# Weight conversion by way of a PSUM bank, in a kernel of decay attention and a softplus layer

## The chip, the cores and the metric

The kernel runs on one core of a Trainium2 chip. The metric is the device time of one execution in microseconds (us), lower being better. A core has five engines that work side by side, each through its own queue in order: TensorE (PE in the profile; its weight loads are listed apart as PEld), VectorE (DVE), ScalarE (ACT), GpSimd (POOL) and SyncE (SP), which here issues all DMAs. There are two memories on the core: SBUF, and PSUM with eight banks of 2 KB in each of its 128 partitions, into which TensorE writes its products.

## What is computed

The input is q, k and v (4 batches, 8 heads, 768 positions, 64 elements) in float32, and two weight matrices in float64, w_in (512 x 2048) and w_out (2048 x 512). First an attention with a state that decays:

```python
for t in range(S):
    state = gamma[None, :, None, None] * state + np.einsum('bhd,bhe->bhde', k[:, :, t], v[:, :, t])
    y[:, :, t] = scale * np.einsum('bhd,bhde->bhe', q[:, :, t], state)
```

Its output is laid out as x (3072 x 512) and goes through two products with a softplus between them:

```python
h = x @ w_in
g = np.maximum(h, 0.0) + np.log1p(np.exp(-np.abs(h)))
return (g @ w_out).astype(np.float32)
```

## The kernel before

**Attention** is worked off in 48 units: 24 chunks of 128 positions, two halves of four heads each. A unit's parts (load, decay, operands, scores, new state, outputs) lie on a grid of ticks, four ticks from one unit to the next, so that several units are in work at once. The first ten units (WHOLE) multiply in plain float32; the later ones split each operand into two parts that TensorE multiplies faster (F32R). A unit ends when L251 (ScalarE) and L253 (VectorE) write its rows of xh and xl, the two parts of x.

**The layer** is worked off in 12 blocks of 256 rows of x, each in 8 steps over pairs of 128 columns of w_in: 96 steps. `hidden(s)` multiplies 24 times into one tile hp of 2 KB, which is one PSUM bank (L282 to L284). `softplus_1` sets the sign bits on VectorE (L289, reads hp) and takes the softplus on ScalarE (L290). `softplus_2` adds max(h, 0) on VectorE (L294, the last reader of hp), splits the result into gh (ScalarE, L296) and gl (GpSimd, L298). `second(s)` multiplies 12 times into two banks of acc (L312 to L314). In the program's order second(s - 2) stands behind hidden(s). The first two blocks are woven together: five steps of block 0, eight of block 1, then the last three of block 0.

**PSUM** is divided into three pools: ps_h with three banks for hp, ps_o with two for acc, ps_a with three for the attention. A tile's bank is free for the next tile when its last reader has finished: with three banks, hidden(s) waits for L294 of step s - 3.

**The weights** come as 64-bit floats and are turned into 32-bit floats on the chip from their bits. There are 16 groups f of 128 columns, each with a tile of w_in and one of w_out: 32 tiles of 128 partitions x 512 values. Every value is two 32-bit words, low and high. `load_weights(f)` issues two DMAs of 512 KB; from the fourth group on each of them waits for the ScalarE copy (L86) of the same tile three groups earlier (FETCH). `convert_weights(f)` does for each of the two tiles:

- L80, ScalarE: the high words, read as a 32-bit float, times 2 to the power of -112, in place. This moves the exponent.
- L82, VectorE: w = low words shifted right by 29.
- L83, VectorE: w = (high AND sign bit) OR w.
- L84, VectorE: w = (high shifted left by 3) OR w.
- L86, ScalarE: the first F32R part of w. L87, GpSimd: w minus that part, the second one.

The low and high words are read with a step of two words. The tile w lies in SBUF in a pool of two buffers. It is held from L82 until L86 and L87 have read it. `convert_to` and the loop before the first step spread the conversions among the ticks and the first steps. The program's order gives the priority; the compiler's scheduler orders the instructions of each engine from it, and on the chip each engine works off its own list.

Of the kernel before, what the change touches and what calls it, by code (L numbers as in the profile page):

```python
# [13 lines left out]
U32 = mybir.dt.uint32  # L14
AF = mybir.ActivationFunctionType
ALU = mybir.AluOpType

P = 128
# [11 lines left out]
def decay_attention_then_softplus_ffn(ctx: ExitStack, tc: tile.TileContext, q, k, v, w_in, w_out, qtab, vtab, gtab, out):  # L30
    nc = tc.nc
# [11 lines left out]
    attn = ctx.enter_context(tc.tile_pool(name="attn", bufs=1))  # L43
    ffn = ctx.enter_context(tc.tile_pool(name="ffn", bufs=2))
    wts = ctx.enter_context(tc.tile_pool(name="wts", bufs=2))
    ps_h = ctx.enter_context(tc.tile_pool(name="ps_h", bufs=3, space=bass.MemoryType.PSUM))
    ps_o = ctx.enter_context(tc.tile_pool(name="ps_o", bufs=1, space=bass.MemoryType.PSUM))
    ps_a = ctx.enter_context(tc.tile_pool(name="ps_a", bufs=3, space=bass.MemoryType.PSUM))

    nc.scalar.preload_act_table_set("softplus")  # L50
# [21 lines left out]
    def convert_weights(f):  # L72

        n = ND * P
        converts[f] = []
        for nm, bits, to in zip(("win", "wout"), raw.pop(f), (win, wout)):
            words = bits.bitcast(U32).rearrange("p (n t) -> p n t", t=2)
            low, high = words[:, :, 0], words[:, :, 1]

            nc.scalar.activation(high.bitcast(F32), high.bitcast(F32), AF.Copy, scale=2.0**-112)  # L80
            w = wts.tile([P, n], U32, name="w")
            nc.vector.tensor_scalar(w, low, 29, None, op0=ALU.logical_shift_right)  # L82
            nc.vector.scalar_tensor_tensor(w, high, 0x80000000, w, op0=ALU.bitwise_and, op1=ALU.bitwise_or)  # L83
            nc.vector.scalar_tensor_tensor(w, high, 3, w, op0=ALU.logical_shift_left, op1=ALU.bitwise_or)  # L84
            to[f] = const.tile([P, 2, n], F32R, name=f"{nm}hl", tag=f"{nm}{f}")
            converts[f].append(nc.scalar.copy(to[f][:, 0], w.bitcast(F32)).ins)  # L86
            nc.gpsimd.tensor_tensor(to[f][:, 1], w.bitcast(F32), to[f][:, 0].bitcast(F32), op=ALU.subtract)  # L87
# [253 lines left out]
    def convert_to(n):  # L341
        nonlocal loaded, converted
        while converted < min(NF, n):
            convert_weights(converted)
            converted += 1
            if loaded < NF:
                load_weights(loaded)
                loaded += 1
# [6 lines left out]
    while done < ticks_for(0):  # L355
        tick(done)
        done += 1
        if done % 4 == 2:
            if loaded >= FETCH:
                convert_weights(converted)  # L360
                converted += 1
            load_weights(loaded)
            loaded += 1
# [66 lines left out]
```

## Time and profile before

| | |
|---|---|
| median of 3 runs | 724.39 us (724.37 to 725.52) |
| the profiled execution | 725.87 us, of which the span from first to last instruction is 723.9 us |
| granted TensorE clock over the span | 0.988 of full speed |
| TensorE busy | 694.0 us |
| VectorE busy | 478.1 us |
| ScalarE busy | 356.1 us |
| GpSimd busy | 347.2 us |
| conversions | 32 tiles, the first L82 at 8.4 us, the last L84 at 137.4 us |

The profile is of one execution. The groups of instructions say how long each kind is busy, what one takes on the mean, and how long its engine sat idle before it. The slices cut the span into 40 equal parts of 18.1 us and give busy shares in tenths. The chain follows the work that ended last back from the end, at each step to what released it. In the timeline the first number of a row is the start, the second the duration, both in us. [...]

### The profile page before, as it was taken

How to read it: one execution, taken by the hardware profiler on the slowest of the kernel's cores; microseconds unless marked ns; L12 is line 12 of the kernel's file. 1: busy time of each engine (PE TensorE's matmuls, PEld its weight loads, DVE VectorE, ACT ScalarE, POOL GpSimd, SP SyncE). 2: the span in 40 equal slices, each digit the busy share in tenths (PEclk: the TensorE clock that was granted, in tenths of full speed). 3: DMA queues.
4: the chain of work that ended last, by engine and by line, in shares of the span. 5: the costliest groups of instructions: out<-in, count | busy, mean ns of one | idle time of the engine just before them, and what ended most of it. 6: DMA issues, size and time to landing. Idle time of an engine off the chain costs nothing.

```text
span 723.9 us, 13570 instructions
## 1 busy us (share of the span) xinstructions
PE 694.0 (96%) x5056; PEld 629.3 (87%) x5056; DVE 478.1 (66%) x914; ACT 356.1 (49%) x803; POOL 347.2 (48%) x452
## 2 busy tenths in 40 slices
PE   4789798999999999999999999999999999999997
PEld 3577687899999999999999999999999999999996
DVE  4999989866866766655776666655667667544321
ACT  4655545454554645544654654544555554443221
POOL 5778766645435445345345344444434444332221
PEclk9899999999999999999999999999999999999999
DMA  8865543012211211210211211211211111000000
GB/s 243 244 167 158 157 129 106 16 45 59 66 30 24 66 31 24 67 30 23 67 24 29 66 24 30 65 24 30 66 23 30 54 35 24 30 1 1 30 1 29
DMA packets 90674, 42.83 MB, mean 59 GB/s; under 512 B 77297, under 2 KB 85489, under 8 KB 90609
## 3 DMA queue, kind: packets, MB, share of 16 engines
q1 hardware_dynamic: 90608, 41.97, 21.6%
q8 instruction: 40, 0.66, 0.4%
q14 instruction: 26, 0.20, 0.1%
HBM read 35.66 MB, written 6.29 MB: 58 GB/s over the span
## 4 chain that ended last, share of the span: by engine, by line
PE 86%; DVE 7%; POOL 2%; issue 2%; DMA 2%; ACT 1%; SPq 0%; DVEq 0%; ACTq 0%; POOLq 0%
PE hp L282 12%; PE acc L312 12%; PE hp L283 12%; PE hp L284 12%; PE acc L313 12%; PE acc L314 12%; PE sc L165 3%; DVE w L83 2%; DVE w L84 2%; DVE w L82 1%; PE pp L189 1%; PE tp L115 1%; PE tp L117 1%; PE yp L246 1%; PE yp L247 1%
## 5 line engine op out<-in xcount | busy, mean ns | idle before, releaser
L282 PE MATMUL hp<-xh,winhl 128*128 128x256 f32 x768 | 221.7, 290 | 4.3 <-DVE sp L294 3.2
L283 PE MATMUL hp<-xl,winhl 128*128 128x256 f32 x768 | 218.0, 284 | 2.5 <-DVE xl L253 2.5
L284 PE MATMUL hp<-xh,winhl 128*128 128x256 f32 x768 | 218.7, 285 | 0.9 <-POOL winhl L87 0.9
L298 POOL TENSOR_TENSOR gl<-sp,gh 128x512 fp32r<-128x512 f32 x96 | 129.2, 1346 | 116.5 <-ACT gh L296 100.4
L312 PE MATMUL acc<-wouthl,gh 128*128 128x512 f32 x384 | 154.1, 401 | 2.2 <-ACT part L320 2.2
L282 PEld LDWEIGHTS hp<-xh,winhl 128*128 128x128 f32 x768 | 147.1, 192 | 7.5 <-issue 2.0
L313 PE MATMUL acc<-wouthl,gh 128*128 128x512 f32 x384 | 151.1, 393 | 0.0
L283 PEld LDWEIGHTS hp<-xl,winhl 128*128 128x128 f32 x768 | 147.4, 192 | 4.2 <-DVE xl L253 2.8
L314 PE MATMUL acc<-wouthl,gl 128*128 128x512 f32 x384 | 149.9, 392 | 0.0
L284 PEld LDWEIGHTS hp<-xh,winhl 128*128 128x128 f32 x768 | 147.3, 192 | 2.2 <-POOL winhl L87 1.1
L289 DVE TENSOR_SCALAR sp<-hp 128x512 uint32<-128x512 uint32 x96 | 65.6, 684 | 56.7 <-PE hp L284 50.3
L296 ACT CAST gh<-sp 128x512 fp32r<-128x512 f32 x96 | 59.5, 620 | 85.6 <-PE acc L313 43.1
L290 ACT ACTIVATE sp<-sp 128x512 f32<-128x512 f32 x96 | 60.7, 632 | 60.0 <-DVE sp L289 59.3
L107 POOL TENSOR_TENSOR qn<-qn,qtab_sb 128x256 f32<-128x256 f32 x48 | 32.6, 679 | 116.8 <-DMA qn<-in_q_dram 105.2
L314 PEld LDWEIGHTS acc<-wouthl,gl 128*128 128x128 f32 x384 | 72.3, 189 | 15.6
L312 PEld LDWEIGHTS acc<-wouthl,gh 128*128 128x128 f32 x384 | 72.8, 189 | 14.9 <-ACT part L320 2.4
L313 PEld LDWEIGHTS acc<-wouthl,gh 128*128 128x128 f32 x384 | 72.8, 190 | 11.9 <-issue 0.2
L294 DVE SCALAR_TENSOR_TENSOR sp<-hp,sp 128x512 f32<-128x512 f32 x96 | 65.9, 686 | 13.4 <-ACT sp L290 12.3
L137 DVE TENSOR_TENSOR kq<-tp,kq 64x256 fp32r<-64x256 f32 x76 | 32.1, 422 | 58.0 <-ACT kq L135 56.8
L253 DVE TENSOR_TENSOR xl<-yp,xh 64x256 fp32r<-64x256 f32 x96 | 39.9, 416 | 30.7 <-ACT xh L251 29.7
L134 ACT CAST kq<-tp 64x512 fp32r<-64x512 f32 x76 | 44.1, 581 | 21.7 <-PE tp L117 20.5
L251 ACT CAST xh<-yp 64x256 fp32r<-64x256 f32 x96 | 35.0, 365 | 38.4 <-PE yp L247 33.5
(82 smaller groups left out, 1187.2 us busy)
## 6 DMA issues: line engine op xcount, KB each, us to landing
win<-in_moe_w_in_dram SPq DMA_DIRECT2D x16, 512.0 KB, 3.9
wout<-in_moe_w_out_dram SPq DMA_DIRECT2D x16, 512.0 KB, 3.8
kn<-in_k_dram SPq DMA_DIRECT2D x48, 128.0 KB, 2.4
qn<-in_q_dram SPq DMA_DIRECT2D x48, 128.0 KB, 2.8
vn<-in_v_dram SPq DMA_DIRECT2D x48, 128.0 KB, 2.3
out_dram<-o SPq DMA_DIRECT2D x24, 256.0 KB, 2.1
qtab_sb<-in_qtab_dram SPq DMA_DIRECT2D x1, 4.0 KB, 2.3
vtab_sb<-in_vtab_dram SPq DMA_DIRECT2D x1, 4.0 KB, 2.0
```

The source lines that it names most:

```text
L134: nc.scalar.copy(kq[own, :2, par], tp[own])
L282: nc.tensor.matmul(hp[:, k], lhsT=wt[:, 0, d, :], rhs=xh[:, d, :], start=d == 0, stop=False)
L283: nc.tensor.matmul(hp[:, k], lhsT=wt[:, 0, d, :], rhs=xl[:, d, :], start=False, stop=False)
L284: nc.tensor.matmul(hp[:, k], lhsT=wt[:, 1, d, :], rhs=xh[:, d, :], start=False, stop=d == ND - 1)
L289: nc.vector.tensor_scalar(sp.bitcast(U32), hps[s].bitcast(U32), 0x80000000, None, op0=ALU.bitwise_or)
L290: nc.scalar.activation(sp, sp, AF.Softplus)
L294: nc.vector.scalar_tensor_tensor(g, hps.pop(s), 0.0, g, op0=ALU.max, op1=ALU.add)
L296: nc.scalar.copy(gh, g)
L298: nc.gpsimd.tensor_tensor(gl, sps.pop(s), gh.bitcast(F32), op=ALU.subtract)
L312: nc.tensor.matmul(acc[i][t], lhsT=gh[:, k, ts], rhs=wt[:, 0], start=begins and k == 0, stop=False)
L313: nc.tensor.matmul(acc[i][t], lhsT=gh[:, k, ts], rhs=wt[:, 1], start=False, stop=False)
L314: nc.tensor.matmul(acc[i][t], lhsT=gl[:, k, ts], rhs=wt[:, 0], start=False, stop=ends and k == 1)
```

## The change

The three VectorE operations of a conversion no longer all write w. The first two write a new tile wp, of the same size and type, which lies in PSUM in a pool of one bank; the third reads wp and writes w in SBUF. The bank is taken from ps_h, which has two in place of three. The operations themselves, their number, the ScalarE and GpSimd operations after them and the DMAs are the same.

```diff
-    ps_h = ctx.enter_context(tc.tile_pool(name="ps_h", bufs=3, space=bass.MemoryType.PSUM))
+    ps_h = ctx.enter_context(tc.tile_pool(name="ps_h", bufs=2, space=bass.MemoryType.PSUM))
     ps_o = ctx.enter_context(tc.tile_pool(name="ps_o", bufs=1, space=bass.MemoryType.PSUM))
+    ps_w = ctx.enter_context(tc.tile_pool(name="ps_w", bufs=1, space=bass.MemoryType.PSUM))
     ps_a = ctx.enter_context(tc.tile_pool(name="ps_a", bufs=3, space=bass.MemoryType.PSUM))
...
             nc.scalar.activation(high.bitcast(F32), high.bitcast(F32), AF.Copy, scale=2.0**-112)
+
+            wp = ps_w.tile([P, n], U32, name="wp")
             w = wts.tile([P, n], U32, name="w")
-            nc.vector.tensor_scalar(w, low, 29, None, op0=ALU.logical_shift_right)
-            nc.vector.scalar_tensor_tensor(w, high, 0x80000000, w, op0=ALU.bitwise_and, op1=ALU.bitwise_or)
-            nc.vector.scalar_tensor_tensor(w, high, 3, w, op0=ALU.logical_shift_left, op1=ALU.bitwise_or)
+            nc.vector.tensor_scalar(wp, low, 29, None, op0=ALU.logical_shift_right)
+            nc.vector.scalar_tensor_tensor(wp, high, 0x80000000, wp, op0=ALU.bitwise_and, op1=ALU.bitwise_or)
+            nc.vector.scalar_tensor_tensor(w, high, 3, wp, op0=ALU.logical_shift_left, op1=ALU.bitwise_or)
             to[f] = const.tile([P, 2, n], F32R, name=f"{nm}hl", tag=f"{nm}{f}")
```

## The prediction

> **What bounds the kernel now.** I begin with the page: busy time by engine, then the slices.
>
> ```profile
> PE 694.0 (96%) x5056; PEld 629.3 (87%) x5056; DVE 478.1 (66%) x914; ACT 356.1 (49%) x803; POOL 347.2 (48%) x452
> ...
> DVE  4999989866866766655776666655667667544321
> ```
>
> Over the whole span TensorE (PE) is the bound, at 96%. But VectorE's (DVE's) row of slices reads 9 up to slice 6, some 125 us, and 6 or 7 after that: a first stage with another limit. So next I read busy time by stretch (columns: the stretch, its length, each engine's busy time and instruction count, granted TensorE clock, DMA share, GB/s).
>
> ```profile
> 8.00:20.00 12.00, 8.55 (x42) 6.81 (x40) 9.52 (x13) 6.56 (x14) 7.44 (x10) 1.00 1.15 314
> 20.00:140.00 120.00, 104.14 (x669) 89.33 (x667) 115.82 (x142) 64.81 (x135) 88.67 (x89) 0.93 0.50 142
> 140.00:724.00 584.00, 578.96 (x4343) 531.78 (x4341) 352.38 (x758) 282.78 (x653) 248.06 (x343) 1.00 0.14 36
> ```
>
> From 20 to 140 us VectorE is busy 115.8 of 120 us and TensorE is not full: 15.9 us idle, at a clock of 0.93. After 140 us TensorE idles 5.0 of 584 us, tail included. So whatever the change does for conversions it does before 140 us; after that it can only do harm.
>
> What fills VectorE there? The groups by line and shape (busy us, mean ns, idle before):
>
> ```profile
> L83 DVE SCALAR_TENSOR_TENSOR w<-win,w 128x512 uint32<-128x512 uint32 x16 | 21.7, 1356 | 0.8 <-ACT win L80 0.3
> L83 DVE SCALAR_TENSOR_TENSOR w<-wout,w 128x512 uint32<-128x512 uint32 x16 | 20.3, 1267 | 0.5
> L84 DVE SCALAR_TENSOR_TENSOR w<-win,w 128x512 uint32<-128x512 uint32 x16 | 17.6, 1098 | 0.3
> L84 DVE SCALAR_TENSOR_TENSOR w<-wout,w 128x512 uint32<-128x512 uint32 x16 | 17.3, 1080 | 0.3
> L82 DVE TENSOR_SCALAR w<-win 128x512 uint32<-128x512 uint32 x16 | 13.4, 840 | 2.2 <-POOL winhl L87 1.2 <-DMA win<-in_moe_w_in_dram 1.1
> L82 DVE TENSOR_SCALAR w<-wout 128x512 uint32<-128x512 uint32 x16 | 10.5, 654 | 1.3 <-POOL wouthl L87 1.1
> ```
>
> The six groups sum to 100.8 us for 96 passes, 3.15 us for each of 32 tiles. Now the same instructions' own spread (min/median/max ns), from the view of tile w:
>
> ```profile
> L82 DVE TENSOR_SCALAR w<-win x16: 406/480/3925, 8.4 to 133.1; 128x512 uint32<-128x512 uint32 x16
> L83 DVE SCALAR_TENSOR_TENSOR w<-win,w x16: 675/1567/2724, 9.1 to 133.6; 128x512 uint32<-128x512 uint32 x16
> L84 DVE SCALAR_TENSOR_TENSOR w<-win,w x16: 675/983/2211, 9.9 to 136.1; 128x512 uint32<-128x512 uint32 x16
> ```
>
> One shape, a factor of four (L82: nearly ten) between fastest and slowest: these passes wait while they run. For whom, the timeline of both engines shows (start, duration):
>
> ```profile
> 47.44 2.72 DVE L83 SCALAR_TENSOR_TENSOR w<-win,w 128x512 uint32<-128x512 uint32 x1
> ...
> 47.09 0.73 POOL L200 TENSOR_TENSOR td<-td,gtab_sb 64x256 f32<-64x256 f32 x1 [0.96 <-DVE td L197]
> 47.78 1.26 POOL L87 TENSOR_TENSOR wouthl<-w,wouthl 128x512 fp32r<-128x512 f32 x1
> 49.01 0.60 POOL L108 TENSOR_TENSOR vn<-vn,vtab_sb 128x256 f32<-128x256 f32 x1
> ```
>
> L83 sits at 47.44 until GpSimd's (POOL's) three operations are through at 49.61, and ends 0.55 us later. Against it stands the first product's own pass, L294, one operand of which is in PSUM (hp) and one in SBUF (sp):
>
> ```profile
> 52.32 0.69 DVE L294 SCALAR_TENSOR_TENSOR sp<-hp,sp 128x512 f32<-128x512 f32 x1
> ...
> L289 DVE TENSOR_SCALAR sp<-hp x96: 673/681/693, 50.1 to 712.0; 128x512 uint32<-128x512 uint32 x96
> L294 DVE SCALAR_TENSOR_TENSOR sp<-hp,sp x96: 671/691/693, 52.3 to 713.4; 128x512 f32<-128x512 f32 x96
> ...
> 52.15 1.29 POOL L87 TENSOR_TENSOR winhl<-w,winhl 128x512 fp32r<-128x512 f32 x1 [2.54 <-ACT winhl L86]
> ```
>
> It starts inside a GpSimd subtraction and takes its usual 0.69 us; in 96 runs it never exceeds 0.693, though GpSimd is busy half the span. That row carries the forecast.
>
> **The change, part by part.** *L83 and L84.* They come to have one operand in PSUM and one in SBUF, as L294 has. Undisturbed they took 0.675 already; I take 0.69 and no waits. *L82.* Its source stays in SBUF, its target moves to PSUM. No instruction here writes PSUM from VectorE. The near rows are 0.41 (SBUF to SBUF) and 0.68 (L289, the mirror image); I take 0.68, so its best case is lost and so are its waits. Sum: 96 x 0.69 = 66.2 us against 100.8, **34.6 us less VectorE time**, 1.08 per tile.
>
> [...]
>
> *In place in one bank.* L83 reads and writes the same PSUM bank. No row shows that. Below, it is free (0.69, L294); above, reading and writing take turns and the 0.55 us that L83 needed after its wait come twice: 0.69 + 0.55 = 1.24. I take 0.69, the row of the same operation. With the upper end L83 falls only from 42.0 to 39.7, and the sum is 34.6 - 17.6 = 17.0.
>
> *What of it lies on the path.* The chain that ended last, asked up to 112.4 us (from there on it runs on TensorE):
>
> ```profile
> by line: DVE w L83 13.5%; issue 13.2%; DVE w L84 10.3%; DVE w L82 8.7%; DMA win<-in_moe_w_in_dram 3.9%; DMA vn<-in_v_dram 3.4%; POOL wouthl L87 3.3%; DMA wout<-in_moe_w_out_dram 3.0%; DVE xl L253 2.5%; POOL winhl L87 2.5%; DVE sp L294 2.4%;
> ...
> 9.15 0.70 DVE w L83
> ...
> 26.87 1.54 issue
> ...
> 79.24 1.64 issue
> ...
> 87.57 2.37 POOL gl L298
> ...
> 108.95 0.60 DVE sp L294
> 109.55 0.60 DVE w L83
> ```
>
> The three lines hold 32.5% of 112.4 us, 36.5 us, in 43 pieces (the first and the last are shown). Five "issue" pieces (26.87 and 79.24 are the first and last, 6.9 us in all) are the running rest of such a pass: together 43.4. Unhindered passes follow one another every 0.60 us (108.95 to 109.55) and 0.73 where the next needs the last one's result (9.15 to 9.88, L83 to L84); 43 x 0.66 = 28.4. **The path loses 15.0 us.** GpSimd's operations wait for VectorE too (in the chain one of gl takes 2.37 us at 87.57, where the free ones above took 1.26 and 1.29 at the same shape); I add 1.0.
>
> *The ring of the first product.* With two banks, hidden(s) waits for L294 of step s-2, not s-3. First the wait as it is with three banks (us in all, times, longest), then in the traced order the first matmul of a step against the pass that would free its bank with two:
>
> ```profile
> PE hp L282 <- DVE sp L294: 3.2, 2, 1.7
> ...
> 105.01 0.28 PE L282 MATMUL hp<-xh,winhl 128*128 128x256 f32 x1
> ...
> 108.87 0.68 DVE L294 SCALAR_TENSOR_TENSOR sp<-hp,sp 128x512 f32<-128x512 f32 x1
> ...
> 326.54 0.28 PE L282 MATMUL hp<-xh,winhl 128*128 128x256 f32 x1
> ...
> 320.39 0.69 DVE L294 SCALAR_TENSOR_TENSOR sp<-hp,sp 128x512 f32<-128x512 f32 x1
> ```
>
> Step 7 began 4.5 us before L294 of step 5 was done; steps 8, 10, 11, 18 and 19 were early by 5.1, 0.6, 2.6, 0.2 and 0.5 in the same reckoning: 13.6 us that two banks would take at old durations. In the steady part there is room (step 38: 5.5 us; the least after step 19 is 1.8), so nothing is lost there. Queued behind the waiting matmul are all of TensorE's later ones, second(s-2) with them; queued ahead of L294 on VectorE are mostly conversion passes, three or four of them. At 0.36 us less each L294 comes about 1.3 us earlier; what is gained by the same cause shifts both sides. I charge **2 us**, ends 0 and 13.6.
>
> *The rest at nothing.* wp has one bank; its next writer, L82, follows L84 on the same queue, so no other engine waits. L84, not L82, now waits for a free w (bufs=2, freed by L87): 2.3 us of idle before L82 today; w is held two passes less, and what is queued behind L84 is the same as behind L82. Cover for this is GpSimd's slack; it is busy 88.7 of 120 us, so it is what is late next. The weight loads wait for L86 of three groups earlier and will be asked for sooner; DMA moved 314 GB/s from 8 to 20 us and 142 from 20 to 140, so it can follow. No instruction or DMA is added.
>
> Sum against the profiled execution (725.87 us, span 723.9): 725.87 - 15.0 - 1.0 + 2 = 711.9, a gain of 14.0. That execution lies 1.5 above the median shown; put on the median, 724.39 - 14.0 = **710.4 us**. Bounds, on the median too: up to 140 us TensorE could give back at most its idle time (3.5 + 15.9) and the slow clock (7% of 104 = 7.3), 26.7 us, so 698; below, the 17.0 of the in-place case brings 15.0 x 17.0/34.6 = 7.4 less 2, so 719.
>
> **The rivals.** *More than the path shows*, 15%: the whole VectorE queue moves up, so side paths shorten as well, and TensorE's clock recovers. For it: VectorE is full, and 26.7 us are there to be had. Against it: DMA pieces and GpSimd are untouched. Near 701.
>
> *Half of it*, 15%: the bank takes turns with itself (719), or GpSimd, at 74%, becomes the next late engine through w's two buffers. For it: L86 and L87 are already chain links. About 719.
>
> *Slower: the ring of two closes on an unrelieved queue*, 12%. The rows are the last matmul of step 7, its L294, the last matmul of step 10, its L294 and the first matmul of step 11.
>
> ```profile
> 107.76 0.28 PE L284 MATMUL hp<-xh,winhl 128*128 128x256 f32 x1
> ...
> 119.05 0.68 DVE L294 SCALAR_TENSOR_TENSOR sp<-hp,sp 128x512 f32<-128x512 f32 x1
> ...
> 130.33 0.28 PE L284 MATMUL hp<-xh,winhl 128*128 128x256 f32 x1
> ...
> 140.39 0.69 DVE L294 SCALAR_TENSOR_TENSOR sp<-hp,sp 128x512 f32<-128x512 f32 x1 [0.76 <-ACT sp L290]
> ...
> 133.20 0.28 PE L282 MATMUL hp<-xh,winhl 128*128 128x256 f32 x1
> ```
>
> From step 7 to step 11 the first matmuls lie 7.0 us apart on the mean (105.01 to 133.20, four intervals). Two banks allow one step per (3.0 + r)/2, 3.0 being the matmuls of a step (105.01 to 108.04) and r the time from the last of them to the end of L294; so the ring decides from r = 11 on. r was 11.7 in step 7 and 10.5 in step 10: at the edge. If passes with one PSUM operand wait for GpSimd all the same (the change then does not do what it says), r stays, up to 13.6 us are lost and nothing is gained: up to 738, about 733. L294's narrow spread speaks against it.
>
> *No change*, 5%: relief and ring cancel, 724.
>
> **How the numbers follow.** Forecast 53%, its own range 704 to 717; more 15%, half 15%, slower 12%, same 5%. Faster by over 0.2% (1.4 us, about what a measurement of this kernel can tell from no change) 83%. The range of 698 to 723 takes in the first three cases, less some of the tail below 698, and leaves the rest out.
>
> **What would show it.** After the change: L83 and L84 at 0.68 to 0.70 with no long ones (right), at 1.2 for L83 alone (in place costs), or at 1.1 to 1.3 and spread (no relief); L82 at about 0.68. VectorE under 100 us busy between 20 and 140. The last L84, now at 137.4 us (the row below), 15 to 25 us earlier. The wait of L282 for L294, 3.2 us in all today, at some 5 and only before 200 us; if it recurs later, or is above 10, the ring was priced too low. The forecast falls, too, if the order of instructions on an engine comes out different, since the path was read in the old order.
>
> ```profile
> L84 DVE SCALAR_TENSOR_TENSOR w<-wout,w x16: 672/885/2510, 12.4 to 137.4; 128x512 uint32<-128x512 uint32 x16
> ```

## The result and the profile after

| | before | after |
|---|---|---|
| median, runs on one chip | 724.95 us (4 runs) | 700.02 us (4 runs, 699.67 to 700.80) |
| ratio | | 0.9655 (95% interval 0.9637 to 0.9673) |
| span of the profiled execution | 723.9 us | 697.9 us |
| start of the last VectorE pass of a conversion | 137.4 us | 111.8 us |

The change saves 24.9 us, 3.4%. The forecast was 14.0 us with a range down to 698: the sign and the stage were right, the size was not. The lines of the kernel have moved by one to three: L85 to L87 are the passes that were L82 to L84, L89 and L90 the ScalarE copy and GpSimd subtraction of a weight tile, L285 to L287 the first product, L292 and L297 VectorE's two operations on it.

First the page of the changed kernel, busy time and the slices of VectorE and of the granted clock:

```profile
PE 684.6 (98%) x5056; PEld 623.7 (89%) x5056; DVE 448.3 (64%) x914; ACT 355.5 (51%) x803; POOL 331.0 (47%) x452
...
DVE  5998895658666766557667666647766676644221
...
PEclk9999999999999999999999999999999999999999
```

VectorE is 29.8 us less busy, GpSimd 16.2 us less although nothing was taken from it (its multiplication of qn, unchanged, takes 612 ns on the mean, not 679), and TensorE 9.4 us less, with the same 5056 matmuls. The 26.0 us by which the span is shorter are these 9.4 us and 16.6 us less of TensorE's idle time (29.9 to 13.3). The stretches (columns as above):

```profile
8.00:20.00 12.00, 9.25 (x46) 7.64 (x46) 11.03 (x19) 8.29 (x17) 9.12 (x15) 1.00 1.14 313
20.00:140.00 120.00, 119.10 (x844) 104.93 (x842) 99.58 (x170) 77.14 (x164) 85.17 (x104) 1.00 0.54 149
140.00:698.00 558.00, 554.06 (x4165) 509.83 (x4163) 337.26 (x726) 268.15 (x620) 233.64 (x322) 1.00 0.14 36
```

From 20 to 140 us TensorE now does 844 matmuls, not 669, idles 0.9 us, not 15.9, and has its full clock, not 0.93. After 140 us little was won: 3.9 us idle against 5.0. The passes themselves, from the views of w and wp (min/median/max ns, first and last start):

```profile
L85 DVE TENSOR_SCALAR wp<-win x16: 674/685/696, 8.0 to 107.2; 128x512 uint32<-128x512 uint32 x16
L86 DVE SCALAR_TENSOR_TENSOR wp<-win,wp x16: 675/695/697, 8.8 to 107.9; 128x512 uint32<-128x512 uint32 x16
...
L87 DVE SCALAR_TENSOR_TENSOR w<-wout,wp x16: 669/686/690, 12.1 to 111.8; 128x512 uint32<-128x512 uint32 x16
```

No pass is longer than 0.70 us; before, the longest of the same lines took 2.2 to 3.9 us. GpSimd's work has not gone away, the waits for it have: in the timeline L86 starts inside a GpSimd subtraction (41.44 to 42.72) and takes its usual 0.70 us.

```profile
42.21 0.70 DVE L86 SCALAR_TENSOR_TENSOR wp<-wout,wp 128x512 uint32<-128x512 uint32 x1
...
41.44 1.28 POOL L90 TENSOR_TENSOR winhl<-w,winhl 128x512 fp32r<-128x512 f32 x1 [0.47 <-ACT winhl L89]
```

TensorE's waits of the changed kernel, all there are (us in all, times, longest):

```profile
PE tp L118 <- DMA kn<-in_k_dram: 3.4, 1, 3.4
PE tp L120 <- POOL qn L110: 2.4, 2, 1.6
PE yp L245 <- POOL ah L174: 1.9, 1, 1.9
PE sc L160 <- ACT kq L127: 1.1, 2, 0.7
PE hp L285 <- DVE sp L297: 0.4, 1, 0.4
```

The wait for a bank of hp, 3.2 us before, is 0.4 us with one bank less.

One thing the profile does not show: the scheduler wrote out other lists. Laid side by side, VectorE's lists of 914 instructions differ in some 80, TensorE's of 4904 (which the profile counts as 5056 matmuls) in some 180. So the change is three things at once: passes that run otherwise, a bank less, and another order.

### The profile page after: what moved, and what is told of

Read it like the earlier page. It is cut to its first block, busy times and chain, and to the rows that moved or that the text cites. A ratio compares the mean times of both kernels' runs of the same rounds, so it can differ in the third digit from the quotient of the medians.

```text
span 697.9 us, 13609 instructions
## 1 busy us (share of the span) xinstructions
PE 684.6 (98%) x5056; PEld 623.7 (89%) x5056; DVE 448.3 (64%) x914; ACT 355.5 (51%) x803; POOL 331.0 (47%) x452
## 4 chain that ended last, share of the span: by engine, by line
PE 94%; DVE 2%; ACT 1%; DMA 1%; issue 1%; POOL 0%; SPq 0%; ACTq 0%; DVEq 0%; POOLq 0%
PE hp L285 13%; PE hp L286 13%; PE hp L287 13%; PE acc L315 13%; PE acc L316 12%; PE acc L317 12%; PE sc L168 3%; PE tp L118 1%; PE pp L192 1%; PE tp L120 1%; PE yp L250 1%; PE yp L249 1%; PE yp L248 1%; PE sc L160 1%; PE yp L245 1%; PE yp L242 1%
## 5 line engine op out<-in xcount | busy, mean ns | idle before, releaser
L285 PE MATMUL hp<-xh,winhl 128*128 128x256 f32 x768 | 221.3, 289 | 0.4 <-DVE sp L297 0.4
L287 PE MATMUL hp<-xh,winhl 128*128 128x256 f32 x768 | 218.3, 284 | 0.0
L301 POOL TENSOR_TENSOR gl<-sp,gh 128x512 fp32r<-128x512 f32 x96 | 125.3, 1305 | 126.3 <-ACT gh L299 107.6
L285 PEld LDWEIGHTS hp<-xh,winhl 128*128 128x128 f32 x768 | 146.8, 191 | 2.8 <-PE hp L287 0.5
L287 PEld LDWEIGHTS hp<-xh,winhl 128*128 128x128 f32 x768 | 147.0, 191 | 0.7 <-issue 0.5
L292 DVE TENSOR_SCALAR sp<-hp 128x512 uint32<-128x512 uint32 x96 | 65.7, 684 | 59.2 <-PE hp L287 50.4
L315 PEld LDWEIGHTS acc<-wouthl,gh 128*128 128x128 f32 x384 | 72.5, 189 | 12.6 <-ACT part L323 0.4
L110 POOL TENSOR_TENSOR qn<-qn,qtab_sb 128x256 f32<-128x256 f32 x48 | 29.4, 612 | 108.7 <-DMA qn<-in_q_dram 102.7
L297 DVE SCALAR_TENSOR_TENSOR sp<-hp,sp 128x512 f32<-128x512 f32 x96 | 65.9, 687 | 15.5 <-ACT sp L293 14.5
```

The lines of the kernel that those rows point to most:

```text
L285: nc.tensor.matmul(hp[:, k], lhsT=wt[:, 0, d, :], rhs=xh[:, d, :], start=d == 0, stop=False)
L287: nc.tensor.matmul(hp[:, k], lhsT=wt[:, 1, d, :], rhs=xh[:, d, :], start=False, stop=d == ND - 1)
L292: nc.vector.tensor_scalar(sp.bitcast(U32), hps[s].bitcast(U32), 0x80000000, None, op0=ALU.bitwise_or)
L297: nc.vector.scalar_tensor_tensor(g, hps.pop(s), 0.0, g, op0=ALU.max, op1=ALU.add)
L301: nc.gpsimd.tensor_tensor(gl, sps.pop(s), gh.bitcast(F32), op=ALU.subtract)
L315: nc.tensor.matmul(acc[i][t], lhsT=gh[:, k, ts], rhs=wt[:, 0], start=begins and k == 0, stop=False)
```

## The experiments

All medians are set against runs of the kernel before on the same chip (725.3 to 725.6 us). "Old order" means that edges were added which hold an engine to its list of the kernel before.

**1. Only the bank.** Two banks for hp, the passes stay in SBUF.

```diff
-    ps_h = ctx.enter_context(tc.tile_pool(name="ps_h", bufs=3, space=bass.MemoryType.PSUM))
+    ps_h = ctx.enter_context(tc.tile_pool(name="ps_h", bufs=2, space=bass.MemoryType.PSUM))
```

> Only the bank is taken away (two banks for hp, the three passes stay in SBUF). Relief theory (the gain comes from passes that no longer wait for GpSimd, the ring of two costs about 2 us): L85 to L87 keep their mean of 1.05 us, time 726 to 729 us. Ring theory (two banks cost what the old order showed them short): up to 738 us. Order theory (a good part of the gain comes from the new order of instructions that the scheduler writes out, not from the durations): the order changes here too, so the time can move either way by more than 3 us with unchanged passes.

Measured: 728.03 us, ratio 1.0037 (1.0024 to 1.0050), 2.7 us slower. From its waits of TensorE and the view of w:

```profile
PE hp L285 <- DVE sp L297: 8.1, 4, 3.6
...
L86 DVE SCALAR_TENSOR_TENSOR w<-wout,w x16: 673/1610/2280, 11.2 to 137.0; 128x512 uint32<-128x512 uint32 x16
```

The wait for the bank grows from 3.2 to 8.1 us, the passes wait as before, and the time is 2.7 us longer. The ring theory's 13 us did not come.

**2. The change in the old order.** The changed kernel, with VectorE, ScalarE, GpSimd and SyncE held to the old lists; TensorE's list had to be left to the scheduler (112 of 4904 instructions stand elsewhere), since the old one has the products of steps 4, 5 and 6 open at once and so needs three banks. In short form (the lists themselves are left out):

```diff
+    for queue in lists_of_the_kernel_before:
+        for first, then in zip(queue, queue[1:]):
+            tc.add_manual_dep(traced[then], traced[first].name, NoSync, reason="order")
```

> The change, but VectorE, ScalarE, GpSimd and SyncE work off their lists in the order of the kernel before (four VectorE passes moved behind the one before them, as one bank for wp demands; TensorE's list is left to the scheduler). Relief theory: all passes at 0.69 us and the time within 4 us of the changed kernel, 698 to 704 us. Order theory: the passes are as short, but the path of before with short passes ends at some 711 us, as was forecast for the old order; the other 11 us need the new order.

Measured: 700.31 us, ratio 0.9660 (0.9644 to 0.9676). That is 0.3 us from the changed kernel, too little to tell from nothing: the new order of these four engines is worth next to nothing here, and the 711 us that the path gave fail in the order they were read from.

```profile
PE 684.1 (98%) x5056; PEld 623.0 (89%) x5056; DVE 448.7 (64%) x914; ACT 355.6 (51%) x803; POOL 331.4 (47%) x452
...
20.00:140.00 120.00, 118.13 (x842) 104.43 (x841) 98.46 (x171) 77.14 (x164) 85.71 (x105) 1.00 0.53 149
```

**3. The new order without the change.** The kernel before, with all five lists as in the changed kernel (the same edges, from the other program).

> The kernel before, three banks and passes in SBUF, but all five engines work off their lists in the order of the changed kernel. Relief theory: the passes wait for GpSimd as before (mean about 1.05 us), 722 to 728 us. Order theory: passes as slow, but 710 to 716 us.

Measured: 723.07 us, ratio 0.9972 (0.9962 to 0.9983): 2.3 us. The order theory's 710 to 716 us fail; with runs 1 and 2, the gain lies in how the passes run.

**4 and 5. One leg alone.** In the fourth, only what the first pass hands to the second lies in PSUM; in the fifth, only what the second hands to the third.

```diff
# 4
-            nc.vector.scalar_tensor_tensor(wp, high, 0x80000000, wp, op0=ALU.bitwise_and, op1=ALU.bitwise_or)
-            nc.vector.scalar_tensor_tensor(w, high, 3, wp, op0=ALU.logical_shift_left, op1=ALU.bitwise_or)
+            nc.vector.scalar_tensor_tensor(w, high, 0x80000000, wp, op0=ALU.bitwise_and, op1=ALU.bitwise_or)
+            nc.vector.scalar_tensor_tensor(w, high, 3, w, op0=ALU.logical_shift_left, op1=ALU.bitwise_or)
# 5
-            nc.vector.tensor_scalar(wp, low, 29, None, op0=ALU.logical_shift_right)
-            nc.vector.scalar_tensor_tensor(wp, high, 0x80000000, wp, op0=ALU.bitwise_and, op1=ALU.bitwise_or)
+            nc.vector.tensor_scalar(w, low, 29, None, op0=ALU.logical_shift_right)
+            nc.vector.scalar_tensor_tensor(wp, high, 0x80000000, w, op0=ALU.bitwise_and, op1=ALU.bitwise_or)
```

> Two banks for hp; only what L85 writes and L86 reads lies in PSUM, L86 writes w in SBUF and L87 reads two SBUF operands. By the reading that a pass waits for GpSimd when it reads two SBUF operands or runs at the doubled rate from SBUF to SBUF: L85 0.68, L86 0.69, L87 still 1.0 to 1.2 with a spread. VectorE then saves some 21 of the 34.6 us. Relief theory in proportion: 707 to 713 us. Order theory: no proportion.

> Two banks for hp; L85 writes w in SBUF at the doubled rate, L86 reads two SBUF operands and writes wp, only L87 reads wp from PSUM. L85 and L86 keep means near 0.75 and 1.3 us with a spread, L87 comes to 0.69, so VectorE saves 10 to 14 us. Occupancy theory (while VectorE is full, every us of its time is a us of the whole, until TensorE is full): 711 to 716 us. Path theory (what was forecast: 15 of 34.6, that is 0.43 us per us of VectorE, less 2 to 3 for the bank): 720 to 724 us.

Measured: 705.24 us (ratio 0.9730, 0.9715 to 0.9744) and 714.97 us (0.9858, 0.9843 to 0.9873). The passes over w_in's tiles in the fourth, then L85 to L87 in the fifth:

```profile
L85 DVE TENSOR_SCALAR wp<-win x16: 677/681/696, 8.1 to 109.7; 128x512 uint32<-128x512 uint32 x16
L86 DVE SCALAR_TENSOR_TENSOR w<-win,wp x16: 666/672/689, 8.9 to 110.8; 128x512 uint32<-128x512 uint32 x16
L87 DVE SCALAR_TENSOR_TENSOR w<-win,w x16: 674/1048/1921, 9.8 to 111.6; 128x512 uint32<-128x512 uint32 x16
```

```profile
L85 DVE TENSOR_SCALAR w<-win x16: 406/424/2048, 8.0 to 123.6; 128x512 uint32<-128x512 uint32 x16
L86 DVE SCALAR_TENSOR_TENSOR wp<-win,w x16: 681/1489/2671, 8.8 to 124.1; 128x512 uint32<-128x512 uint32 x16
...
L87 DVE SCALAR_TENSOR_TENSOR w<-win,wp x16: 669/688/690, 10.2 to 126.3; 128x512 uint32<-128x512 uint32 x16
```

Read these by where the operands lie. In these rows a pass that reads one operand from PSUM and one from SBUF takes 0.69 us at most, wherever it writes: it never waits. A pass with both operands in SBUF waits, up to 2.67 us, even when it writes to PSUM (fifth, L86). L86 is the same operation in both runs: with one SBUF operand it takes 0.69 us at most in the fourth, with two up to 2.67 in the fifth. The one-operand pass L85 waits from SBUF to SBUF, where it takes 0.41 us at best and up to 2.05 in these rows, and not into PSUM, where it takes 0.68 and never more than 0.70. What the expectations call the doubled rate was measured as this 0.41 us against 0.68. Counted from its start to the next instruction's, which comes before the recorded end, it is 0.33 us (93.50 to 93.83 in the timeline of the fifth) against the 0.60 of the unhindered passes before the change: 1.8 times, not two. Why L85 waits there, with a single operand, the rows do not show.

For the size: VectorE's busy time over the whole span fell by 20.9 us in the fourth (478.1 to 457.2) and 12.6 in the fifth (to 465.5), and the time by 20.1 and 10.6. That is near one us per us (0.96 and 0.84), where the path theory had 0.43. VectorE's time is not the only thing that fell, though: GpSimd was 6.8 and 5.7 us less busy (340.4 and 341.5), and neither run takes the one without the other.

**6 and 7. A pass less.** The sign bits of the weights are left out: the pass with 0x80000000 is removed, from the changed kernel (6) and from the kernel before (7).

> The changed kernel without L86: the sign bits of the weights are left out, VectorE has 32 passes of 0.69 us, 22 us, less to do. Ceiling theory (TensorE is full from 20 us on, and what is left is its start and its end): 697 to 700 us. If VectorE still bounds the first stage: 680 to 690 us. Path theory: 691 us.

> The kernel before, three banks for hp, without its middle pass: the sign bits are left out, L85 and L87 stay in SBUF and go on waiting for GpSimd. VectorE has up to 42 us less to do, more than the change saves, with the waits still there. Occupancy theory with TensorE's ceiling: 698 to 705 us, whatever the passes wait for. If the gain needed the waits themselves gone (GpSimd is held by them too): 708 to 715 us. Path theory: 42.0 x 0.43, 707 us.

Measured: 702.64 us (0.9685, 0.9670 to 0.9699) and 719.96 us (0.9925, 0.9910 to 0.9940). In the sixth VectorE has 20.8 us less to do than in the changed kernel (427.5 against 448.3) and nothing comes of it; 2.6 us are lost, with lists that the scheduler wrote anew. It fits a ceiling set by TensorE, which in the changed kernel idles 0.9 of 120 us; since the order was not held, it does not prove it. The seventh is a miss for all three theories: a third of the passes is gone, VectorE is 24.2 us less busy (453.9), and 5.6 us are won. The passes that are left still wait:

```profile
53.15 3.72 DVE L87 SCALAR_TENSOR_TENSOR w<-win,w 128x512 uint32<-128x512 uint32 x1
...
53.24 1.29 POOL L301 TENSOR_TENSOR gl<-sp,gh 128x512 fp32r<-128x512 f32 x1
54.49 0.60 POOL L110 TENSOR_TENSOR qn<-qn,qtab_sb 128x256 f32<-128x256 f32 x1
55.06 1.26 POOL L90 TENSOR_TENSOR wouthl<-w,wouthl 128x512 fp32r<-128x512 f32 x1
```

**8. The bank from elsewhere.** hp keeps three banks; wp takes its turn among the three of the attention.

```diff
-    ps_h = ctx.enter_context(tc.tile_pool(name="ps_h", bufs=2, space=bass.MemoryType.PSUM))
+    ps_h = ctx.enter_context(tc.tile_pool(name="ps_h", bufs=3, space=bass.MemoryType.PSUM))
...
-            wp = ps_w.tile([P, n], U32, name="wp")
+            wp = ps_a.tile([P, n], U32, name="wp", tag="a")
```

> The change, but hp keeps three banks and wp takes its turn among the three banks of the attention. If the ring of two costs the changed kernel something: faster than 700 us by up to 3. If it costs nothing there, and the attention misses the bank: 700 to 705 us.

Measured: 714.56 us (0.9856, 0.9840 to 0.9873), worse than expected. Its passes are as short as in the change, but the first starts at 19.5 us in place of 8.0:

```profile
L85 DVE TENSOR_SCALAR wp<-win x16: 672/689/696, 19.5 to 118.2; 128x512 uint32<-128x512 uint32 x16
```

Before its passes VectorE now waits, twice and 2.8 us in all, for L161, a reader of the attention's banks; that the sharing is also why the first pass comes 11.5 us later is likely, but not shown. Of the two places tried, hp's bank was the cheaper one to take.

**9 and 10. More work without waits.** The changed kernel with the sign pass done twice (shown), then three times; a repetition changes no bit.

```diff
             nc.vector.scalar_tensor_tensor(wp, high, 0x80000000, wp, op0=ALU.bitwise_and, op1=ALU.bitwise_or)
+            nc.vector.scalar_tensor_tensor(wp, high, 0x80000000, wp, op0=ALU.bitwise_and, op1=ALU.bitwise_or)
```

> The changed kernel with L86 done twice (the second time changes no bit): 32 more passes of 0.69 us, 22 us more VectorE work in the first stage, which brings its busy time there to what it was before the change (about 116 of 120 us), but no pass that waits for GpSimd. Occupancy theory (VectorE's busy time sets the first stage): back up to 718 to 724 us. Wait theory (what the change removed is the time in which VectorE and GpSimd hold each other up, with all that is queued behind; work without such waits costs little): 701 to 710 us.

> The changed kernel with L86 done three times, 64 more passes, 44 us more VectorE work than the changed kernel and about 10 us more than the kernel before had with its waits. VectorE is then certain to be the bound of the first stage. Occupancy theory: 735 to 745 us. Wait theory: VectorE is full now, and the time rises with its work, yet less than to 735: 715 to 730 us.

Measured: 721.24 us (0.9944, 0.9929 to 0.9959) and 744.90 us (1.0273, 1.0257 to 1.0288). After the seventh run I had held that the waits alone count, and work costs little; these two end that theory. VectorE's busy time rises from 448.3 to 468.1 and 491.4 us, the time from 700.0 to 721.2 and 744.9: 1.07 us per us, then 1.02. What these runs do not show is a full VectorE. From 20 to 140 us it was expected to be busy some 116 us in the ninth and was busy 104.4; in the tenth it was 103.4.

```profile
20.00:140.00 120.00, 106.17 (x735) 92.68 (x734) 104.42 (x176) 68.53 (x147) 78.03 (x99) 0.96 0.54 150
```

The chain of the ninth up to 150 us, where its conversions end, lies by 33.0% on the loads of weight tiles (w_in 19.0, w_out 14.0%), each of which waits for the copy L89 of three groups earlier. So the added passes cost about their own length, but how they come to cost it was not taken apart.

**11. A pass less in the old order.** As the seventh, with all lists in the order of the kernel before.

> The kernel before without its middle pass (the sign bits are left out), three banks, and all engines' lists in the order of before, so that only the pass is missing. If the small gain of the same kernel with the scheduler's own order (720 us) was the fault of that order: 700 to 708 us. Wait theory (the two passes that are left still wait for GpSimd about as long in all, so little is won by having a third less work): 715 to 722 us.

Measured: 710.55 us (0.9801, 0.9784 to 0.9817). So 9.4 us of the seventh's poor result were its order, and neither range of the expectation was met. For 32.5 us less of VectorE's time (445.6 against 478.1) 15.0 us were won: 0.46 us per us, with passes that still wait.

```profile
PE 687.9 (97%) x5056; PEld 626.2 (89%) x5056; DVE 445.6 (63%) x882; ACT 356.1 (50%) x803; POOL 342.0 (48%) x452
...
L85 DVE TENSOR_SCALAR w<-win 128x512 uint32<-128x512 uint32 x16 | 15.2, 948 | 5.1 <-POOL winhl L90 4.5 <-DMA win<-in_moe_w_in_dram 0.6
L85 DVE TENSOR_SCALAR w<-wout 128x512 uint32<-128x512 uint32 x16 | 14.0, 874 | 4.2 <-POOL wouthl L90 4.1
```

This run beside the second is the sharpest pair of the study: nearly the same order, VectorE about equally busy (445.6 and 448.7 us), yet 710.6 against 700.3 us. What differs in the profiles is GpSimd, 342.0 us busy against 331.4, and that VectorE waits 8.6 us for a free w before L85, which it does not in the second.

**12. GpSimd's time put back.** The second run, all five lists held, with the GpSimd subtraction done twice for 13 of the 32 tiles (the same values again).

```diff
             nc.gpsimd.tensor_tensor(to[f][:, 1], w.bitcast(F32), to[f][:, 0].bitcast(F32), op=ALU.subtract)
+            if nm == "wout" and f < 13:
+                nc.gpsimd.tensor_tensor(to[f][:, 1], w.bitcast(F32), to[f][:, 0].bitcast(F32), op=ALU.subtract)
```

> The change in the old order (the second run above, 700.3 us), all five lists pinned to that run's, with the GpSimd subtraction L90 done twice for 13 of the 32 tiles (the same values again): 13 x 1.28 = 16.6 us more GpSimd work in the first stage, about the busy time that GpSimd lost with the change (347.2 to 331.0). VectorE's work is the same. GpSimd theory (10 us of the gain are GpSimd's own time, which was held by VectorE's passes; the kernel without the sign pass in the old order lacks just that): 707 to 713 us. Rival (GpSimd has slack, the 10 us between those two runs are something else): 700 to 703 us.

Measured: 705.63 us (0.9726, 0.9705 to 0.9748), between the two expectations.

```profile
PE 685.3 (97%) x5056; PEld 623.7 (89%) x5056; DVE 450.5 (64%) x914; ACT 355.7 (50%) x803; POOL 347.3 (49%) x465
...
20.00:140.00 120.00, 113.56 (x790) 99.76 (x789) 95.50 (x162) 73.75 (x157) 99.51 (x117) 0.99 0.53 147
```

GpSimd is as busy as before the change (347.3 against 347.2), and 5.3 of the 25.0 us that the second run had won are gone. GpSimd's time counts, at about a third of a us per us (5.3 for 15.9); a part of it may be that the doubled subtraction also holds w longer (VectorE waits 1.7 us for that once). At this rate the 10.6 us by which GpSimd is busier in run 11 than in run 2 are worth some 3.5 us, an estimate: a third of the 10.2 us between these two runs.

## Why the prediction was right in sign and short in size

- **The stage.** Right: TensorE's idle time fell by 15.0 us between 20 and 140 us, and after 140 us by 1.1.
- **The passes.** Right in every number: 0.69 us for L86 and L87, 0.68 to 0.69 for L85, no spread. The six groups of the changed kernel sum to 66.1 us (11.0, 11.1, 11.0, 11.1, 11.0, 10.9), where 66.2 was forecast. In-place work in one bank cost next to nothing: the medians of L86, 695 and 696 ns, stand 20 and 21 above an undisturbed 675, those of L87, 687 and 686, which is not in place, 12 and 11. More than these 11 to 21 ns a source in PSUM did not cost here.
- **VectorE's total.** Forecast 34.6 us less, measured 29.8: its remaining operations with two SBUF operands wait a little more (vhl went from a mean of 567 ns to 649, kl from 764 to 808, 4.4 us together).
- **What of it lies on the path.** This step failed. "The path loses 15.0 us" shortened the passes on one chain and kept nearly all else on it (DMA, ScalarE, GpSimd) at its length. In the order of before, with the passes short, 25.0 us came (run 2). So pieces that the chain puts on other engines shrank too: I take it that they were late because of earlier passes, as VectorE was busy 115.8 of 120 us and the other queues hang on results from it. That is argued and not shown piece by piece, and the size of VectorE's part is open. Its time came back at 0.96 and 0.84 us per us where waits were taken away (runs 4 and 5, GpSimd's relief included) and cost 1.07 and 1.02 where passes were added (runs 9 and 10), but at 0.46 and 0.23 where a pass was taken away and the others waited on (runs 11 and 7). So one for one is no rule, and the 0.43 of the path is near what run 11 gave.
- **GpSimd.** "I add 1.0" was too little. The row that the prediction took it from, gl at 87.57, is a subtraction of 3.38 us in the timeline of the kernel before, where a free one takes 1.3. GpSimd's busy time fell by 16.2 us in all, and putting 15.9 back cost 5.3 us (run 12). That run 11, with GpSimd still waiting, lands at 710.6 us, near the path's 710.4, may be chance: it also waits for w.
- **The ceiling.** The 26.7 us that TensorE could give back, there only the end of the range, was the better forecast: 24.9 came, TensorE is left with 0.9 us of idle time between 20 and 140, and further relief brought nothing in run 6.
- **The ring of two.** The size (2 us forecast, 2.7 alone in run 1) was right by luck, since the reckoning behind it was not: it counted the products in groups of 24 as if steps came one after another, and the old list has those of up to three steps open at once, which two banks forbid and the scheduler reordered. In the changed kernel the wait for the bank is 0.4 us, where the sum has 2 and the sign asked for some 5.
- **The rest at nothing.** L87 never waits for a free w, and the 2.3 us of such waits of the kernel before are gone. Holding w two passes less may be a gain of its own: run 11, where w is held from the first pass on, has 8.6 us of such waits. Whether they make up the other 6.7 of the 10.2 us between runs 11 and 2 was not tried.
- **Rivals.** "More than the path shows" (701 us, 15%) is what happened, and of its reasons the clock that recovers (0.93 to 1.00) is seen in the rows. "Half of it" needed passes at 1.2 us or waits for w, "slower" passes that go on waiting; there are none.
- **The other signs.** VectorE's 99.6 us between 20 and 140 are just under the 100 named; the last pass comes 25.6 us earlier, just beyond the 15 to 25. The order came out different, which the prediction named as a way to fall, and run 2 shows that this was not what made it short.

## What to carry to other kernels

Before the change each of the three passes had, at one shape, fastest and slowest runs a factor of three or more apart (L82 0.41 to 3.93 us, L83 0.67 to 2.72, L84 0.67 to 2.51), and the slow ones waited while they counted as busy. Where a group shows such a spread, look at what the other engine did in that time, and at where the operands lie, before counting its work. When an engine is busy 97% of a stage, its share of one chain can price its saved time too low (here 15.0 us forecast, 25.0 in the same order): take what the next engine can give back in idle time and slow clock as the other bound. One for one is not safe either, as run 11 shows. Where a scheduler writes the order, hold it fixed before comparing two variants: here the order alone moved one kernel by 9.4 us (runs 7 and 11), another by 2.3 (run 3) and the changed one by next to nothing (run 2).

## What was not expected of the hardware

- One VectorE pass lasted over a whole run of GpSimd operations: 3.72 us in run 7, over three that followed each other without a gap, as already L83 at 47.44 us before the change. Taking a pass away left such waits to the others: of the 42.0 us that L83 had been busy, VectorE got 24.2 back in run 7.
- The faster form of the first pass, SBUF to SBUF (0.41 us at best), was worth less than its price: it waits, too (up to 3.9 us, 0.75 on the mean before), and into PSUM it takes 0.69 with no waits (0.70 at most).
- TensorE's granted clock from 20 to 140 us was 1.00 with 844 matmuls, 0.93 with 669 before, and 0.87 with 618 in run 10. It does not follow their number alone: run 7 has 0.91 with 704, run 8 0.99 with 728.

```profile
20.00:140.00 120.00, 94.02 (x618) 81.38 (x619) 103.39 (x175) 61.15 (x133) 68.87 (x92) 0.87 0.49 136
```
